# Copying the mixed V of each batch to key order: eight copies of 1 KB pieces in place of sixteen of 512 bytes

## The chip, the core and the metric

The kernel runs on one core of a Trainium2 chip. The metric is the device time of one execution in microseconds (us). Thirteen runs of the kernel before gave a median of 159.22 us, from 157.39 to 160.86. The engines are named as in the profile: PE multiplies matrices, PEld loads its weights, DVE, ACT and POOL work on vectors, SP issues transfers. "SPq" is the queue of SP.

## The reference, cut to what matters

There are 4 batches, 8 heads, a sequence of 768 tokens in 8 blocks of 96, and heads of 64 elements. A matrix P of 8x8 for each head mixes whole blocks of K and V, attention then works inside each block, and the result goes through a gated layer.

```python
k_sorted = np.einsum('bhij,bhjcd->bhicd', P, k_b)
v_sorted = np.einsum('bhij,bhjcd->bhicd', P, v_b)
scores = scale * np.matmul(q_b, k_sb.transpose(0, 1, 2, 4, 3))
attn = softmax(scores)                       # over the 96 keys of a block
x = np.matmul(attn, v_sb)                    # then (B, S, H*D)
h = np.maximum(x @ w_in, 0.0);  u, v = halves of h
v_s = w_spatial @ normalised(v) + b_spatial
out = (u * v_s) @ w_out
```

## The kernel before, in words

A load puts one input of one batch into a tile of 128 partitions: partition p holds tokens 6p to 6p+5 of every head (the six are called g). A block i of 96 tokens is therefore 16 partitions (t) times 6 values of g.

The work is cut into steps, and one string, SCHEDULE, gives their order on PE, DVE, ACT and POOL. A step is a letter, a number, a batch, the engine that empties its result (A for ACT, D for DVE) and a PSUM tile (ps0 to ps3); `v31A1` is step v, number 3, batch 1, emptied by ACT, in ps1. Each engine takes its instructions in that order; SP has an order of its own, in which its transfers were written. The steps that matter here:

- **v** (`vmix`, L260): two matmuls mix the blocks of V for a pair of heads. ACT or DVE copies the result to the tile vm (by the helper at L235 and L237). Batch 0 does the same work in another way (steps t and B) and copies nothing on SP.
- **vb<-vm** (L277, on SP): copies of vm to vb, in which the 96 partitions are the keys of a block. Each takes one block i: 96 pieces. In vm the heads lie in two halves of four, and eight copies for a half start when both pairs of that half are mixed. The order of the pairs is 0, 2, 3, 1 in batch 1, so the half of pairs 2 and 3 goes first, with 0 and 1 after it. In batches 2 and 3 it is 3, 2, 1, 0.
- **s** (`score`, L365, exponential at L372 on ACT) and **z** (`sums`, L384, then L390 and L391 on ACT): scores and their row sums.
- **a** (`attend`, L402): matmuls of vb and the exponentials; DVE multiplies by the reciprocal sums into xt (L412). Step a11 is batch 1, number 1: it reads blocks 4 to 7 of the half with pairs 0 and 1. Steps a01, a21 and a31 follow.
- **V, U, N, S, O**: the gated layer of the batch before, interleaved with attention. S (L494) is followed by an addition on DVE (vs, L505) and a product on POOL (gt, L506); O (L535) reads the four gt.
- **Q** (`qdma`, L309 and L313): for batches 2 and 3, DVE copies q_in to qr and SP issues a transposing transfer to qT.
- **The loads** of batches 2 and 3 (L94, issued by POOL: q_in, then v_in, then k_in) start behind a small copy on POOL ("gate", L596) that waits for the first exponential of the batch before.

Around a11 the order written out is `s71-2 s51-1 S20-3 s31-0 s61-2 S00-1 s11-3 s41-0 S30-2 s21-1 z11-3 Q02-- a11-0 z31-2 z01-1 O10A3 a01-2 z21-0 O00A1 a21-3 a31-2 O20A0 V01-1`. Step S30 is number 3 of the gated layer of batch 0, whose product gt is the last of four that O10, O00 and O20 read.

SP's transfers use eight completion semaphores in turn, so that a transfer waits for the one eight places ahead of it.

Of the kernel before, what the change touches and what calls it, by code (L numbers as in the profile page):

```python
# [9 lines left out]
BF16 = mybir.dt.bfloat16  # L10
# [20 lines left out]
def kernel(  # L31
# [14 lines left out]
    B, H, S, D = q.shape  # L46
    NB = sort_net.shape[-1]
    BLK = S // NB
    G = S // 128
    TB = 128 // NB  # L50
# [6 lines left out]
    HP = H // 2  # L57
# [7 lines left out]
    att = ctx.enter_context(tc.tile_pool(name="att", bufs=2))  # L65
# [13 lines left out]
    def ps_tile(n, dt=FP32):  # L79
        return psum.tile(  # L80
            [128, 2, 512 if dt == FP32 else 1024], dt, name=f"ps{n}", tag=f"ps{n}",
        )
# [9 lines left out]
    def load_heads(x, b, name):  # L92
# [16 lines left out]
        out=a16.rearrange("p (j t) -> p j t", t=TB),  # L109
        in_=a16.rearrange("p (j t) -> p j t", t=TB),  # L110
# [6 lines left out]
        out=sel.rearrange("p i (j t) -> p i j t", t=TB),  # L117
        in_=sel.rearrange("p i (j t) -> p i j t", t=TB),
# [14 lines left out]
        out=w_in_sb.rearrange("p (j x) f -> p j (x f)", x=2),  # L133
        in_=moe_w_in.rearrange("(j p x) f -> p j (x f)", j=2, x=2),
# [98 lines left out]
    def copy(eng, out, in_):  # L233
        if eng is nc.scalar:
            nc.scalar.copy(out=out, in_=in_)  # L235
        else:
            nc.vector.tensor_copy(out=out, in_=in_)  # L237
# [10 lines left out]
    class Attention:  # L248
# [7 lines left out]
        def vmix(self, hp, eng, ps):  # L256
            t = ps_tile(ps)
            for hh in range(2):
                h = 2 * hp + hh
                nc.tensor.matmul(  # L260
                    t[:, hh, 0:G * D], lhsT=self.pd[:, h, :], rhs=v_in[self.b][:, h, :],
                    start=True, stop=True,
                )
            half, h0 = hp // 2, 2 * hp % (H // 2)
            if self.vm is None:
                self.vm = att.tile([128, 2, G, H // 2, D], BF16, name="vm", tag="vm")
            copy(
                eng,
                self.vm[:, half, :, h0:h0 + 2, :].rearrange("p g h d -> p h g d"),
                t[:, :, 0:G * D].rearrange("p h (g d) -> p h g d", g=G),  # L270
            )
            if self.vb is None:
                self.vb = att.tile([BLK, NB, 2, H // 2, D], BF16, name="vb", tag="vb")
            self.mixed.append(hp)
            if hp ^ 1 in self.mixed:
                for i in range(NB):
                    nc.sync.dma_start(  # L277
                        out=self.vb[:, i, half].rearrange("c h d -> c (h d)"),
                        in_=self.vm[i * TB:(i + 1) * TB, half].rearrange("t g h d -> t g (h d)"),
                    )  # L280

        def q_tile(self):
# [282 lines left out]
    with tc.manual_schedule(engines={ET.PE, ET.DVE, ET.Activation, ET.Pool}):  # L565
# [8 lines left out]
        for x in range(1, B):  # L574
            make_pdiag(x, nc.gpsimd, 0, H)
        nc.gpsimd.tensor_copy(
            out=b_bc.rearrange("p (g c) -> p g c", g=G),
            in_=b_nat.rearrange("p (c g) -> p g c", g=G),
        )
        for step in SCHEDULE.split():  # L580
            name, n, b = step[0], int(step[1]), int(step[2])
# [48 lines left out]
```

The softmax here doesn't subtract the row's maximum and nothing guards it: scores larger than these inputs give would overflow.

## Time and profile before

| | us |
|---|---|
| median of 13 runs | 159.22 |
| lowest, highest | 157.39, 160.86 |
| the profiled execution | 159.08 |
| its span, first to last instruction | 157.3 |
| busy: PE, DVE, ACT, POOL | 143.4, 93.8, 94.4, 49.1 |
| mean granted PE clock | 0.983 of full |

The profile is of one execution. "Idle before ... <-releaser" says what ended an engine's wait. The chain that ended last is followed back from the last instruction, at each step to what released it; a piece of it shows its start, its length and its line. DMA issues have a duration on the queue that issues them and a time from issue to landing.

### The profile page before, as it was taken

What the parts mean: (1) busy time and instruction counts of PE and PEld (TensorE: products, weight loads), DVE (VectorE), ACT (ScalarE), POOL (GpSimd) and SP (SyncE); (2) the same over time, 40 slices, a digit from 0 to 9 for tenths busy, and PEclk for the clock granted to TensorE, in tenths of its full rate; (3) what the DMA queues carried; (4) which work ended last, traced back from release to release, by engine and by line L of the source; (5) the groups of instructions that cost most, each with busy time, mean ns of one, the idle gap of its engine ahead of it and who ended that gap; (6) DMA issues with size and microseconds to landing.
All of it is one profiled execution on the core that took longest, in us unless ns stands there. A gap on an engine that the chain in (4) does not pass through costs nothing.

```text
span 157.3 us, 4205 instructions
## 1 busy us (share of the span) xinstructions
PE 143.4 (91%) x1805; PEld 81.7 (52%) x1805; DVE 93.8 (60%) x193; ACT 94.4 (60%) x141; POOL 49.1 (31%) x47
## 2 busy tenths in 40 slices
PE   0968899999999789999999999999999999999970
PEld 0336785557766334455655635456555444566430
DVE  3778976498854422475962765578643855844710
ACT  3156997599755646477986725688875445550060
POOL 7975923000078620000077440000056400007500
PEclk9999999999999968999999999999999999999997
DMA  2999999999959999954469999954510063000055
GB/s 14 190 204 211 216 272 196 201 204 205 183 55 177 213 204 165 301 226 57 72 76 207 205 195 148 356 141 61 77 27 0 6 264 139 0 4 0 0 209 193
DMA packets 27171, 23.09 MB, mean 147 GB/s; under 512 B 7504, under 2 KB 25168, under 8 KB 27024
## 3 DMA queue, kind: packets, MB, share of 16 engines
q0 software_dynamic: 13504, 12.58, 49.7%
q1 hardware_dynamic: 13504, 10.10, 27.3%
q8 instruction: 14, 0.23, 0.6%
q10 hardware_dynamic: 144, 0.13, 0.3%
q14 instruction: 5, 0.04, 0.1%
HBM read 24.78 MB, written 6.29 MB: 198 GB/s over the span
## 4 chain that ended last, share of the span: by engine, by line
PE 49%; DMA 25%; POOL 7%; SPq 7%; DVE 3%; issue 2%; ACT 2%; POOLq 1%; DVEq 0%
DMA v_in<-in_v_dram 16%; PE ps L535 12%; PE ps L478 10%; PE ps L435 10%; PE ps L494 9%; SPq L277 7%; DMA q_in<-in_q_dram 5%; DMA vb<-vm 4%; POOL gt L506 3%; PE ps L260 2%; PE ps L322 2%; DVE vs L505 2%; PE ps L402 1%; PE ps L365 1%; PE ps L521 1%
## 5 line engine op out<-in xcount | busy, mean ns | idle before, releaser
L506 POOL TENSOR_TENSOR gt<-vs,u_sb 128x768 bf16<-128x768 f32 x15 | 25.2, 1687 | 50.0 <-DVE vs L505 26.4
L494 PE MATMUL ps<-wspT,v_sb 128*128 128x384 bf16 x192 | 33.4, 327 | 0.0
L372 ACT ACTIVATE ex<-ps 96x768 bf16<-96x768 f32 x32 | 24.1, 802 | 9.3 <-PE ps L365 8.9
L505 DVE TENSOR_TENSOR vs<-ps,b_bc 128x768 f32<-128x768 f32 (+1 forms) x17 | 15.5, 910 | 20.4 <-PE ps L494 20.4
L457 DVE BATCH_NORM_STATS2 stats<-v_sb 128x6 f32<-128x512 bf16 x24 | 16.2, 675 | 13.3 <-ACT v_sb L241 13.3
L494 PEld LDWEIGHTS <-v_sb 128*128 128x128 bf16 x192 | 17.8, 98 | 12.0 <-issue 0.6
L478 PE MATMUL ps<-xt,w_in_sb 128*128 128x384 bf16 x128 | 23.0, 326 | 0.0
L535 PE MATMUL ps<-w_out_sb,gt 128*128 128x512 bf16 x88 | 22.6, 403 | 0.4
L435 PE MATMUL ps<-w_in_sb,xt 128*128 128x512 bf16 x96 | 22.4, 379 | 0.0
L235 ACT COPY o_sb<-ps 128x1024 f32<-128x1024 f32 x9 | 9.1, 1012 | 20.1 <-PE ps L535 20.1
L412 DVE TENSOR_TENSOR xt<-ps,lns 128x384 bf16<-128x384 f32 x32 | 15.8, 550 | 8.8 <-PE ps L402 8.2
L241 ACT ACTIVATE v_sb<-ps 128x1024 bf16<-128x1024 f32 (+1 forms) x15 | 12.4, 851 | 9.2 <-PE ps L435 9.2
L478 PEld LDWEIGHTS <-w_in_sb 128*128 128x128 bf16 x128 | 12.1, 98 | 8.4
L435 PEld LDWEIGHTS <-xt 128*128 128x128 bf16 x96 | 9.2, 98 | 10.6 <-DVE xt L412 0.4
L535 PEld LDWEIGHTS <-gt 128*128 128x128 bf16 x88 | 8.0, 101 | 11.8 <-POOL gt L506 2.3
L596 POOL COPY gate<-ex 1x1 bf16<-1x1 bf16 x2 | 0.4, 194 | 41.2 <-ACT ex L372 41.2
L241 ACT ACTIVATE u_sb<-ps 128x768 bf16<-128x768 f32 x14 | 11.1, 808 | 1.9 <-PE ps L478 1.5
L390 ACT ACTIVATE lns<-ps 128x384 f32<-128x384 f32 x16 | 7.8, 486 | 6.7 <-PE ps L384 6.7
L365 PEld LDWEIGHTS <-kT 64*96 64x96 bf16 x256 | 7.4, 121 | 4.7 <-issue 3.3
L365 PE MATMUL ps<-qT,kT 64*96 64x96 bf16 x256 | 9.5, 210 | 0.4 <-ACT ex L372 0.4
L237 DVE CAST kT<-ps 128x768 bf16<-128x768 f32 x10 | 9.1, 945 | 0.6 <-PE ps L322 0.6
L402 PE MATMUL ps<-ex,vb 96*32 96x96 bf16 x512 | 8.0, 207 | 1.6 <-DMA vb<-vm 1.6
(80 smaller groups left out, 161.7 us busy)
## 6 DMA issues: line engine op xcount, KB each, us to landing
out_dram<-o_sb SPq DMA_DIRECT2D x11, 512.0 KB, 4.5
q_in<-in_q_dram POOLq DMA_DIRECT2D x4, 768.0 KB, 8.5
k_in<-in_k_dram POOLq DMA_DIRECT2D x4, 768.0 KB, 16.1
v_in<-in_v_dram POOLq DMA_DIRECT2D x4, 768.0 KB, 12.1
vb<-vm SPq DMA_DIRECT2D x48, 48.0 KB, 2.6
wsp_nat<-in_moe_w_spatial_dram POOLq DMA_DIRECT2D x1, 1152.0 KB, 21.3
w_in_sb<-in_moe_w_in_dram POOLq DMA_DIRECT2D x1, 1024.0 KB, 15.6
w_out_sb<-in_moe_w_out_dram POOLq DMA_DIRECT2D x1, 512.0 KB, 30.6
```

What stands on the lines that cost most here:

```text
L241: nc.scalar.activation(out=out, in_=in_, func=AF.Relu)
L277: nc.sync.dma_start(out=self.vb[:, i, half].rearrange("c h d -> c (h d)"), in_=self.vm[i * TB:(i + 1) * TB, half].rearrange("t g h d -> t ...
L365: nc.tensor.matmul(t[0:BLK, hh, ii * BLK:(ii + 1) * BLK], lhsT=self.k[hp][rows, i * BLK:(i + 1) * BLK], rhs=self.q[hp][rows, i], start=Tru ...
L372: nc.scalar.activation(out=e.rearrange("p h i c -> p h (i c)"), in_=t[0:BLK, :, 0:NB // 2 * BLK], func=AF.Exp, scale=scale,)
L412: nc.vector.tensor_mul(out=self.xt[j][:, dh, :].rearrange("p (g i t) -> p i g t", g=G, i=NB)[:, i0:i0 + NB // 2], in0=t[:, dh, 0:HW].rearr ...
L435: nc.tensor.matmul(self.vt[n][:, x, :], lhsT=self.xt(kc)[:, g * 128:(g + 1) * 128], rhs=w_in_sb[:, kc, DH:DFF], start=(kc == 0), stop=(kc ...
L457: nc.vector.bn_stats(out=stats, in_=v_sb[:, x, :])
L478: nc.tensor.matmul(t[:, x, 0:HW], lhsT=w_in_sb[:, kc, mc * 128:(mc + 1) * 128], rhs=self.xt(kc)[:, x * HW:(x + 1) * HW], start=(kc == 0), ...
L494: nc.tensor.matmul(t[:, x, 0:HW], lhsT=self.v[g][:, mc * 128:(mc + 1) * 128], rhs=wspT[:, g, x * HW:(x + 1) * HW], start=(g == 0), stop=(g ...
L505: nc.vector.tensor_add(out=vs[:, x], in0=t[:, x, 0:HW], in1=b2[:, x])
L506: eng.tensor_mul(out=gt2[:, x], in0=vs[:, x], in1=u2[:, x])
L535: nc.tensor.matmul(t[:, x, :], lhsT=self.gt[mc][:, g * 128:(g + 1) * 128], rhs=w_out_sb[:, mc, :], start=(mc == 0), stop=(mc == FC - 1),)
```

## The change

The tile vm keeps its size, but its axes are in another order: first g, then the two halves, then the four heads of a half. For one token all eight heads then lie side by side: 512 elements of two bytes, 1 KB. Copies start when all four pairs of heads are mixed, one for each block, so a batch has 8 copies of 96 KB where it had 16 of 48 KB. In the program that is built, SP's list has 8 copies of 96 pieces of 512 elements where it had 16 of 96 pieces of 256; apart from the numbers of the tiles, the orders of PE, DVE, ACT and POOL are the same. Batch 0 is untouched.

```diff
             if self.vm is None:
-                self.vm = att.tile([128, 2, G, H // 2, D], BF16, name="vm", tag="vm")
+                self.vm = att.tile([128, G, 2, H // 2, D], BF16, name="vm", tag="vm")
             copy(
                 eng,
-                self.vm[:, half, :, h0:h0 + 2, :].rearrange("p g h d -> p h g d"),
+                self.vm[:, :, half, h0:h0 + 2, :].rearrange("p g h d -> p h g d"),
                 t[:, :, 0:G * D].rearrange("p h (g d) -> p h g d", g=G),
             )
             self.mixed.append(hp)
-            if hp ^ 1 in self.mixed:
+            if len(self.mixed) == HP:
                 for i in range(NB):
                     nc.sync.dma_start(
-                        out=self.vb[:, i, half].rearrange("c h d -> c (h d)"),
-                        in_=self.vm[i * TB:(i + 1) * TB, half].rearrange("t g h d -> t g (h d)"),
+                        out=self.vb[:, i].rearrange("c x h d -> c (x h d)"),
+                        in_=self.vm[i * TB:(i + 1) * TB].rearrange("t g x h d -> t g (x h d)"),
                     )
```

## The prediction

> **What bounds the kernel now.** I read four views, in this order. First the page's slices of the span: PE is busy in nine tenths or more almost everywhere, so a copy between tiles is worth something only where PE stands still or slows.
>
> ```profile
> PE   0968899999999789999999999999999999999970
> PEclk9999999999999968999999999999999999999997
> ```
>
> Away from both ends PE dips in one place, the 14th and 15th slices (51.1 to 59.0 us), and there the granted clock falls. Second, the chain of waits through that place:
>
> ```profile
> 42.82 1.83 SPq L277
> ...
> 49.45 6.32 DMA vb<-vm
> 55.77 0.04 issue
> 55.81 0.27 PE ps L402 x8
> 56.08 0.33 PE ps L384 x8
> 56.41 3.52 PE ps L535 x8
> 59.92 0.45 PE ps L402 x32
> ```
>
> The end of the kernel is traced back through step a01 (59.92), step O10 (56.41), the last eight matmuls of a11 (55.81) and the last copy vb<-vm of batch 1, which began to be issued at 49.45 and landed at 55.77. Ahead of it stand all sixteen issues of that batch, from 38.23 on, one of them of 1.83 us. Third, the timeline there:
>
> ```profile
> 53.04 0.35 PE L384 MATMUL ps<-ex,ones 96*32 96x384 bf16 x4
> ...
> 53.85 0.27 PE L402 MATMUL ps<-ex,vb 96*32 96x96 bf16 x8 [0.46 <-DMA vb<-vm]
> 53.95 2.28 POOL L506 TENSOR_TENSOR gt<-vs,u_sb 128x768 bf16<-128x768 f32 x1 [0.97 <-DVE vs L505]
> ...
> 55.81 0.27 PE L402 MATMUL ps<-ex,vb 96*32 96x96 bf16 x8 [0.43 <-DMA vb<-vm]
> ...
> 56.34 3.58 PE L535 MATMUL ps<-w_out_sb,gt 128*128 128x512 bf16 x8
> ```
>
> Step a11 could start at 53.39, when z11 (53.04, 0.35) is through. It waits four times, once for each of its blocks, for the last four copies. O10 then needs 3.52 us for eight matmuls; eight of the same line take 1.83 at 60.54 in the chain. Fourth, the table by stretches says why:
>
> ```profile
> core 0: us, PE busy (x) PEld busy (x) DVE busy (x) ACT busy (x) POOL busy (x), PEclk, DMA share, GB/s
> 53.00:56.40 3.40, 1.78 (x51) 0.74 (x46) 1.93 (x3) 1.81 (x4) 2.28 (x1) 1.00 1.30 209
> 56.40:59.80 3.40, 3.40 (x10) 0.94 (x8) 0.82 (x2) 1.81 (x4) 0.00 (x0) 0.50 1.30 200
> 59.80:63.20 3.40, 3.40 (x110) 1.94 (x110) 1.27 (x3) 2.72 (x4) 0.00 (x0) 1.00 1.29 168
> ```
>
> PE was busy for 1.78 of 3.40 us while it waited for the copies, then had half its clock (0.50) for 3.4 us. The copies are paid twice: in the wait, and in O10.
>
> **The change part by part.** *Issues.* The price of one issue is in the list of vb's instructions:
>
> ```profile
> L277 SPq DMA_DIRECT2D vb<-vm x48: 571/600/1827, 38.2 to 113.3; - x48
> DMA to landing us min/median/max: 2.2/2.6/6.9
> ```
>
> 0.60 us, and 0.04 between two. No copy of 1 KB pieces is in this trace, so its issue is bounded by its neighbours: 0.60 if the 96 pieces set it, 1.2 if the bytes do. The output's issues at L542 move 512 KB in 128 pieces of 4 KB with a median of 0.34 us, more bytes for less time, so I take 0.60. Below 0.57 there is no row of a copy, and no reason for one.
>
> *Start.* The copies now wait for the last of four vm copies. In batch 1 that is ACT's at 39.72, 0.82 long: 40.54, where the first half began at 38.23. Eight issues at 0.64 begin from 40.57 to 45.05. If one of them again takes 1.83 (a fetch of instructions runs in that half microsecond, 42.5 to 43), the last begins at 46.28. Before it began at 49.45.
>
> *Landing.* Between 2.2 and 6.9 us (the row above). The long ones come from the loads of batch 2: these move their first packets at 46 to 47, SP's queue then gets 3 packets between 47 and 50, and about 175 a microsecond from 51 to 54. Most of the copies are issued before that. The last lands at 47.3 (45.05 + 2.2), at the worst 53.2 (46.28 + 6.9); were the landing to double with the bytes, 58.9. I take the first two, both before a11 at 53.39. *A rule on piece size:* a packet of 512 bytes takes about 50 ns here (from 108 to 116 us, 1091 packets for 41.4% of 16 engines: 53 us). The Trainium skill ("DMA: Bandwidth & Descriptors", section "Why small descriptors are slow (HBM only)") says that transfers between SBUF and SBUF don't pay the penalty of small pieces; by that a 1 KB packet takes twice as long, the engines' work for a batch stays the same, and the piece size saves nothing. No row here decides it, and the sum holds either way: six packets an engine are 0.3 to 0.6 us a copy, no more than an issue.
>
> *What is late next.* With vb there, a11's 32 matmuls take 0.51 (the row of 32 at 94.71): 53.39 to 53.90. z31 and z01 take 0.50 (55.91), free to start when DVE and ACT have emptied their PSUM tiles at 53.87 and 53.96: done by 54.46. O10's first six matmuls, at 0.23 each (1.83 / 8), end at 55.84. Its last two need S30's product on POOL, 53.95 + 2.28 = 56.23, and that does not move: DVE's addition before it ends at 53.87 as now. PE resumes about 0.05 later, as behind POOL at 92.23, and 2 x 0.23 brings it to 56.74. a01 started at 59.92: **3.18 us earlier**, 1.69 of it O10's pace (3.52 - 1.83), 1.49 the wait. The clock should hold: from 53.0 to 56.4 PE is then busy for about 2.9 us, not 1.78.
>
> *How far it carries.* From 59.92 to 77.19 the chain is PE without a wait, so all of it moves. What doesn't move with it is early enough: v_in and k_in of batch 2 land at about 58 and 63 (issued at 45.49 and 46.36, 12.5 and 16.6 us), used at 66.56 and 70.33, less 3.18; the transposed q of batch 2 lands at 67.4 (54.80 + 12.6), used at 77.10 less 3.18. Then the chain is the load of q_in for batch 3, 8.12 us from 78.92, behind the gate that waits for batch 2's first exponential: it moves too. DVE waits for that load at 87.06 with the addition of S01 behind it, POOL for that, O21 for POOL at 92.28. In batch 2 the old copies overlap this load (issues to 81.74; 42, 70, 99 and 82 packets of SP's queue in the four microseconds from 82.5, 0.7 us of the engines). The new ones begin at 72.85 and end at 78.0, so it lands 0 to 0.7 earlier; but S31 ends on PE at 89.19, then 0.11 of gap, 0.96 on DVE, 0.07, 1.64 on POOL: 91.97 and not 92.23, so at most 0.3 of it counts. I take 0.15.
>
> *Edits at nothing.* The later start of the first half in batches 2 and 3 is hidden by scores and S steps: copies landed by about 81 and 113, needed at 89.30 and 121.36. Without those 8 us it would cost the 2.3 us that they start later. The copies into vm write runs of 64 elements as before: 0 to 0.01 each. Fewer entries in SP's queue free the transposes and outputs behind them; the transpose at 54.80 waits for qr (54.74), so nothing there. Eight semaphores in turn: the ninth transfer is no longer a copy of the same batch.
>
> **Sum.** 159.08 (span 157.3 and 1.78 around it, which stays) less 3.18 less 0.15 is 155.75. That execution lies 0.14 under the median, so 155.8 stands for a median. Its own error: 0 to 0.3 at q_in, a POOL product that takes 1.64 and not 2.28 (0.44 less, as O10's first six then end last), a wait of some tenths at a11 (0.5 more): 155.2 to 156.4.
>
> **Rivals.** *The clock still falls (17%).* O10 still has a wait of 0.44 before its last two matmuls. For it: half busy was enough for a fall here. Against: 4.68 of 4.90 us busy from 87.40 to 92.30, with the wait for POOL in it, kept 1.00. A fall costs up to 1.69: 157.5. *A rule on the clock:* the trace has gaps of under half a microsecond and a drop to 0.50. The Trainium skill ("TensorE: Matmul & The Clock Gate", section "HAM oscillation — how this bites in real kernels") puts the limit at idle gaps of over 3.4 us; by that the copies didn't cause the drop, it would stay, and the time would be 157.5. The row speaks against it: no such gap stands before 56.4.
>
> *Bytes set the issue, and the first half is now late (9%): slower.* The place is SP's list in batch 1. At p us an issue the last begins at 40.57 + 7p, plus the 1.2 of the long one, and lands 6.3 later among the loads; it beats 55.77 only while p is under 1.1. At 1.24 it lands at 56.8, 1.0 later than now: 160.1. For it: half the copies wait 2.3 us longer than now, and the queue starves from 47 to 50. Against: L542's 0.34.
>
> *Nothing to see (6%).* The build keeps eight copies, but each 1 KB could go as two packets of 512, or the loads come earlier as the queue is empty and starve the last copies as before: the last four land at 55.8 again: 159.2.
>
> **How the numbers follow.** Forecast 68%: 155.8. The range takes in its bounds with half a microsecond of scatter below, and the clock case with as much above (the thirteen runs lie within 1.8 of their median): 154.7 to 158.2; left out are slower and unchanged. A measurement of this kernel can tell about 0.5% from no change. Faster: the forecast and the clock case, 85%; within 0.5%: 6%; slower: 9%.
>
> **What would show it.** Right: 24 issues of L277 of about 0.6 us; no wait of L402 for vb; O10 in about 2.3 us with POOL's gt as its last wait; clock 1.00 from 53 to 63; a01 near 56.7; the gate of batch 3 near 75. Wrong: issues of 1.2 us, or L402 waiting behind 53.4; a clock of 0.50 anywhere but the end; PE idle between 57 and 74, where I count on none.

## The result, and the profile after

The changed kernel takes 156.30 us (median of 11 runs, 156.02 to 156.73); the kernel before has 158.99 in 48 runs by now (156.74 to 160.86). The ratio of times is 0.9893, with a 95% interval of 0.9861 to 0.9925; it compares runs within 1.5% of the fastest of their kernel, which leaves out the 22 longest of the 48, so the medians lie further apart, at 0.983. The prediction was 155.8, with 154.7 to 158.2 as its range. The profiled execution took 155.94 us, with a span of 154.2; the sum was made for 155.75.

The page's slices for PE and its clock, after:

```profile
PE   0978898999999989999999999999999999999970
PEclk9999999999999999999999999999999999999998
```

The dip in the 14th and 15th slices is all but gone, and the clock stays. The chain of waits through the same place (start, length, what):

```profile
53.04 0.97 DVE vs L505
54.01 0.07 issue
54.08 2.30 POOL gt L506
56.38 0.05 issue
56.43 0.60 PE ps L535 x2
57.03 0.46 PE ps L402 x32
```

No copy and no issue of SP is in it any more. It comes through S30's addition and product, and O10's last two matmuls wait for that product. a01 starts at 57.03, not 59.92. The timeline there:

```profile
53.17 0.35 PE L384 MATMUL ps<-ex,ones 96*32 96x384 bf16 x4
...
53.34 0.51 PE L402 MATMUL ps<-ex,vb 96*32 96x96 bf16 x32
...
54.52 1.46 PE L535 MATMUL ps<-w_out_sb,gt 128*128 128x512 bf16 x6
...
56.43 0.60 PE L535 MATMUL ps<-w_out_sb,gt 128*128 128x512 bf16 x2 [0.45 <-POOL gt L506]
```

a11 runs in one piece behind z11. In the table by stretches (columns as before: PE's busy time is the second number, the granted clock the third from the end) PE is busy for 2.78 of the 3.40 us, and the clock stays at 1.00:

```profile
53.00:56.40 3.40, 2.78 (x58) 1.33 (x56) 2.85 (x4) 3.02 (x7) 2.40 (x2) 1.00 1.32 207
56.40:59.80 3.40, 3.37 (x82) 1.62 (x86) 1.02 (x2) 2.70 (x5) 0.00 (x0) 1.00 1.30 199
```

And vb's issues (ns, least, median, most) with their landings:

```profile
L277 SPq DMA_DIRECT2D vb<-vm x24: 576/596/1290, 40.7 to 107.3; - x24
...
DMA to landing us min/median/max: 2.7/3.2/6.8
```

An issue of 96 pieces of 1 KB costs 0.596 us, one of 512 bytes 0.600. The eighth copy of batch 1 is issued from 45.9 to 46.6 and is the one that takes 6.8 us: it lands at about 52.7, some 0.6 us ahead of a11 (53.34).

### The profile page after: what moved, and what is told of

Its sections match the earlier page's. It is cut to its first block, busy times and chain, and to the rows that moved or that the text cites. A ratio compares the mean times of both kernels' runs of the same rounds, so it can differ in the third digit from the quotient of the medians.

```text
span 154.2 us, 4178 instructions
## 1 busy us (share of the span) xinstructions
PE 141.7 (92%) x1805; PEld 81.7 (53%) x1805; DVE 94.2 (61%) x193; ACT 94.2 (61%) x141; POOL 49.0 (32%) x47
## 4 chain that ended last, share of the span: by engine, by line
PE 58%; DMA 29%; POOL 4%; DVE 3%; issue 2%; POOLq 1%; DVEq 0%
DMA q_in<-in_q_dram 29%; PE ps L494 14%; PE ps L535 11%; PE ps L435 10%; PE ps L478 9%; POOL gt L506 4%; PE ps L322 2%; PE ps L365 2%; PE ps L295 2%; PE ps L402 2%; DVE vs L505 2%; PE ps L260 2%; PE ps L521 1%; POOLq L625 1%; PE ps L384 1%
## 5 line engine op out<-in xcount | busy, mean ns | idle before, releaser
L535 PE MATMUL ps<-w_out_sb,gt 128*128 128x512 bf16 x88 | 21.1, 380 | 0.6 <-POOL gt L506 0.5
L468 DVE TENSOR_SCALAR v_sb<-v_sb,mv,rstd 128x512 bf16<-128x512 bf16 x24 | 8.8, 434 | 0.6 <-ACT rstd L466 0.6
```

What stands on the lines that cost most here:

```text
L535: nc.tensor.matmul(t[:, x, :], lhsT=self.gt[mc][:, g * 128:(g + 1) * 128], rhs=w_out_sb[:, mc, :], start=(mc == 0), stop=(mc == FC - 1),)
```

## The experiments

**The theory:** all of the gain is when the copies of blocks 4 to 7 land in batch 1, ahead of a11 or among the loads of batch 2. It comes as a shorter wait (about 1.5 us) and, in most executions, as a clock that doesn't fall (about 1.7). **The main rival:** larger pieces or fewer issues save something of their own, in each batch. One measure is used for all: the time from the start of z11 to the start of a01 in the profiled execution. By the timelines it is 6.81 us before (53.04 to 59.85) and 3.79 after (53.17 to 56.96); where nothing ahead of z11 was changed, its start differs by up to 0.5 us between executions, and this leaves that out. Kernels are compared with runs of the kernel before on the same chip.

**The change in batch 1 alone, and in batches 2 and 3 alone.**

```diff
-            if hp ^ 1 in self.mixed:
+            wide = self.b == 1            # the other kernel: self.b > 1
+            if wide and len(self.mixed) == HP:
...
+            if not wide and hp ^ 1 in self.mixed:
```

(vm has the new order of axes where `wide` holds, and the old one elsewhere.)

> The change in batch 1 alone; batches 2 and 3 copy as before. Theory (the gain is the last copies of batch 1, which land ahead of a11 in place of behind the loads of batch 2): all of it but 0 to 0.3 us at the load of q_in for batch 3, so 156.2 to 156.7, no wait of L402 for vb, clock 1.00 around 57. Rival (a 1 KB piece or half the issues saves something in each batch): a third of the gain, about 158.

> The change in batches 2 and 3 alone. Theory: nothing but 0 to 0.3 us, so 158.7 to 159.3 where the clock drops, with the four waits of a11 for vb as before. Rival (something is saved in each batch): two thirds of the gain, about 157.

Measured: 156.68 (156.54 to 156.89) and 159.51 (157.75 to 160.91), beside 159.19. Batch 1 alone has the gain, 2.51 us between the medians where the change has 2.69, with 3.84 us from z11 to a01; batches 2 and 3 have none (ratio 1.005, 0.9996 to 1.0104). The rival falls. The profile of the second, by stretches, holds one thing more:

```profile
53.00:56.40 3.40, 1.80 (x52) 0.75 (x48) 1.95 (x3) 1.73 (x4) 2.35 (x2) 1.00 1.30 210
56.40:59.80 3.40, 3.35 (x52) 1.58 (x50) 1.81 (x4) 3.30 (x7) 0.00 (x0) 1.00 1.30 201
```

The waits of a11 are those of the kernel before (PE busy for 1.80 us, there 1.78), but in this execution the clock held. From z11 to a01 it took 5.12 us, 1.69 less than the 6.81 of before, and the run was the fastest of its ten. So the same wait is followed by a fall of the clock in some executions and not in others.

The kept traces suggest why. Three of them have a fall of the clock in this place: the kernel before and two kernels further down (sixteen copies after the last mix, five more copies). In each the clock falls once more at the end of the kernel, 98.99 us later (56.38 and 155.37, 56.04 and 155.03, 58.93 and 157.92), which is 29 times the 3.41 us that a fall lasts. The falls thus lie on a grid of 3.41 us, whose place differs from one execution to the next. Counted back from its own fall at the end (153.46), the grid of this execution cuts the wait in two at 54.47, and PE is busy for 79% of the 3.41 us ahead of that and 73% of those behind it. In the kernel before one piece of the grid, 52.97 to 56.38, holds all four waits, with PE busy for 52%. This is read from a few traces; no run here shifts the grid. Nor is the busy share the whole rule: 62% (52.63 to 56.04, sixteen copies after the last mix) was followed by a fall, and 50% near the start of another execution (8.88 to 12.29, the two edits of order below) was not.

**Sixteen copies of 512 bytes in another order.**

```diff
             if hp ^ 1 in self.mixed:
-                for i in range(NB):
+                for i in (4, 5, 6, 7, 0, 1, 2, 3) if self.b == 1 and half == 0 else range(NB):
```

> The kernel before, with sixteen copies of 512 bytes; only the list of the last eight copies of batch 1 begins with blocks 4 to 7, which a11 reads, and ends with 0 to 3. Theory (when these four land is all that counts): they are issued from 44.75 to 47.3, land by about 53, and most of the gain is there without fewer issues or larger pieces: 156.2 to 157.0. Rival (fewer issues and larger pieces free the transfer engines or SP's queue): 159, as before.

Measured: 156.31 (156.18 to 156.58), as fast as the change, beside 159.19. Sixteen issues take 11.88 us of SP as before, and a11 runs without a wait:

```profile
53.59 0.51 PE L402 MATMUL ps<-ex,vb 96*32 96x96 bf16 x32
```

3.78 us from z11 to a01. Neither the size nor the number of the copies is needed for the gain.

**PE kept busy while it waits.** Twenty matmuls of no use, five ahead of each block of a11:

```diff
                 i = ih * (NB // 2) + ii
+                for _ in range(5 if self.b == 1 and m == 1 else 0):
+                    nc.tensor.matmul(t[:, 0, 384:512], lhsT=ident_bf, rhs=warm_sb[:, 0:128],
+                                     start=True, stop=True)
```

> The kernel before, with five matmuls of no use (128x128, into columns of PSUM that nothing reads) in front of each of a11's four blocks, so that PE isn't idle while it waits for the copies. The waits stay, the copies land as before. Theory (half of the gain is the clock, which falls because PE is half busy in those 3.4 us): O10 runs at full pace, about 1.7 us less where the clock fell, 157.3 to 157.8, and the runs lie closer together than those of before. Rival (the clock falls for another reason, or only idle gaps of over 3.4 us make it fall): 159 or more, with the clock at 0.50 from 56.4.

Measured: 157.82, and all ten runs lie from 157.20 to 158.06. By stretches:

```profile
53.00:56.40 3.40, 3.38 (x73) 2.06 (x72) 1.95 (x3) 1.74 (x4) 2.43 (x2) 1.00 1.30 211
56.40:59.80 3.40, 3.35 (x52) 1.58 (x50) 1.81 (x4) 3.30 (x7) 0.17 (x1) 1.00 1.30 202
```

a11's blocks still start some 0.6 us apart, at 54.04, 54.63, 55.21 and 55.89; only PE is busy in between. The 48 runs of the kernel before fall in two groups, 14 from 156.74 to 157.76 and 34 from 158.57 to 160.86, with none between; of the 19 beside this kernel five lie from 157.13 to 158.02 and fourteen from 158.79 up. With the filling only the lower group is left, so it is PE's idle time in the wait that makes the upper one. That each of the 34 has the fall of the clock is inferred: of the kernel before one execution was profiled, and the mean granted clock of a whole run doesn't part the groups (beside this kernel 0.974 to 0.986 in the fourteen and 0.982 to 0.984 in four of the five). Nor is the gap between the groups there in the runs beside later experiments, some of which lie from 158.00 to 158.41.

**Sixteen copies, written after the last mix.**

```diff
-            if hp ^ 1 in self.mixed:
+            if len(self.mixed) == HP:
                 for i in range(NB):
-                    nc.sync.dma_start(out=self.vb[:, i, half]...
+                    for half in range(2):
+                        nc.sync.dma_start(out=self.vb[:, i, half]...
```

> The layout of before and sixteen copies of 512 bytes, but all of them issued only when all four pairs are mixed, block by block with both halves of a block in turn: the start of the change without its smaller number of issues. Theory (the number of issues in SP's list sets when the last copies land): block 7 is issued at about 49.5 to 51, among the loads, and lands at 56 to 57; the gain is gone, 159.0 to 160.4 where the clock falls. Rival (the later start, or which half goes first, is what helped): 156.5.

Measured: 157.03 (156.44 to 159.43), beside 158.54. This didn't do what it says. SP's list isn't the order in which the transfers are written (as the section on the kernel puts it): what can start stands first. In the built list six copies of the half that was ready come first (from 38.42), and those of the other half for blocks 4, 5, 6 and 7 stand in places 11, 12, 13 and 15, where they had 13 to 16. Accordingly the first two blocks of a11 don't wait:

```profile
53.39 0.42 PE L403 MATMUL ps<-ex,vb 96*32 96x96 bf16 x16
...
54.12 0.27 PE L403 MATMUL ps<-ex,vb 96*32 96x96 bf16 x8 [0.31 <-DMA vb<-vm]
...
55.40 0.27 PE L403 MATMUL ps<-ex,vb 96*32 96x96 bf16 x8 [1.01 <-DMA vb<-vm]
```

Seven of ten runs took 156.4 to 157.4, with a mean granted clock of 0.991 to 0.999, three 158.4 to 159.4, with 0.982 to 0.984. It says nothing on a late start; as a dose between before and after it fits the theory.

**No loads of batch 2.** Its steps read the tiles of batch 1, so part of the output comes from other inputs.

```diff
+                    if b == 1:
+                        q_in[2], v_in[2], k_in[2] = q_in[1], v_in[1], k_in[1]
+                        continue
```

> The kernel before without the loads of q, v and k of batch 2: its steps read the tiles of batch 1, so part of the output is that of other inputs. Theory (the loads of batch 2 are what makes the last copies of batch 1 take 6.3 us to land): they land in 2.2 to 3 us, at 52.5 at the latest, a11 doesn't wait and the clock stays: 155.8 to 156.5, with all sixteen issues in place. Rival (SP's sixteen issues are the limit, whatever the loads do): 159.

Measured: 156.64 (156.41 to 157.60), beside 158.54. Sixteen issues as before. The landings of vb's copies, and then a11 in the timeline:

```profile
DMA to landing us min/median/max: 2.2/2.2/6.3
```

```profile
53.29 0.51 PE L402 MATMUL ps<-ex,vb 96*32 96x96 bf16 x32
```

No wait, 3.78 us from z11 to a01. The last seven copies of batch 1, issued from 45.1 on, all land in 2.2 us; in the kernel before they took 6.3 us and more (the 6.3 here is a copy of a later batch). The loads are what the last copies waited behind.

**The changed copies, later.** Two kernels have the change's eight copies of 1 KB pieces, but later. First by moving step v11:

```diff
-        ... w00D1 v11A0 k01D2 k31A3 q01D1 k21A0 q11D2
+        ... w00D1 k01D2 k31A3 q01D1 k21A0 v11A0 q11D2
```

> The changed kernel with step v11, the last pair of V in batch 1, behind k01, k31, q01 and k21 in the order: eight copies of 1 KB pieces as in the change, but issued about 3 us later, from 43.6 to 48. Theory (only the time at which the copies of blocks 4 to 7 land counts): the last ones go into the loads of batch 2 and land at 54.5 to 56, a11 waits for them again, 157.0 to 157.8 where the clock holds and 158.5 to 160 where it falls. Rival (eight issues or 1 KB pieces are the gain in themselves): 156.3.

Measured: 159.11 (157.76 to 161.87), beside 158.83; a11 waits again, three times:

```profile
55.71 0.27 PE L402 MATMUL ps<-ex,vb 96*32 96x96 bf16 x8 [0.40 <-DMA vb<-vm]
...
56.46 0.27 PE L402 MATMUL ps<-ex,vb 96*32 96x96 bf16 x8 [0.48 <-DMA vb<-vm]
...
57.17 0.27 PE L402 MATMUL ps<-ex,vb 96*32 96x96 bf16 x8 [0.44 <-DMA vb<-vm]
```

The waits are as expected, 1.32 us in all, and from z11 to a01 it takes 4.69 us, 0.90 more than in the change, with the clock at 1.00. The time of the whole kernel can't be read: z11 itself starts at 54.84, 1.67 later than in the changed kernel, since v11 waits on PE for its PSUM tile (0.89 us). So SP was pushed back instead, by five copies that nothing reads, with PE's order as in the change:

```diff
+                if self.b == 1:
+                    unread = dram.tile([5, BLK, H * D + 128], BF16, name="unread", tag="unread", bufs=1)
+                    for i in range(5):
+                        nc.sync.dma_start(out=unread[i, :, 0:H * D], in_=...)   # the same 96 x 1 KB
                 for i in range(NB):
```

> The changed kernel with five more copies of 96 pieces of 1 KB from vm in front of those of batch 1 on SP, to a place in memory that nothing reads; the orders of the other engines are the changed kernel's. They push the eight copies of vb back by five issues, 3.2 us, into the loads of batch 2, and leave PE alone, which moving step v11 did not. Theory (the time at which blocks 4 to 7 land is what counts, at its edge: the changed kernel's last copy lands some 0.5 us ahead of a11): a11 waits for vb again for 1 to 3 us, and the time is 157.0 to 158.0 where the clock holds and 158.7 to 160 where it falls. Rival (eight issues, or 1 KB pieces, are the gain in themselves): 156.3 to 156.6.

Measured: 160.82 (160.33 to 161.22), beside 157.72: slower than the kernel before, with all of the change in it.

```profile
44.75 7.17 SPq L284 DMA_DIRECT2D vb<-vm  x8
...
56.29 0.27 PE L409 MATMUL ps<-ex,vb 96*32 96x96 bf16 x8 [2.01 <-DMA vb<-vm]
...
57.02 0.27 PE L409 MATMUL ps<-ex,vb 96*32 96x96 bf16 x8 [0.46 <-DMA vb<-vm]
...
57.72 0.27 PE L409 MATMUL ps<-ex,vb 96*32 96x96 bf16 x8 [0.43 <-DMA vb<-vm]
...
58.52 0.27 PE L409 MATMUL ps<-ex,vb 96*32 96x96 bf16 x8 [0.53 <-DMA vb<-vm]
```

3.4 us of waits and 8.58 from z11 to a01. It is beyond what was expected: the copies were 4 us later, not 3.2 (44.75 against 40.72; 0.76 of that stood ahead of the five, which begin at 41.48), their issues took 7.17 us and not 5.87, landings 7.2 us at the median and 8.3 at most, and the clock fell from 58.93 to 62.34. The five copies' own traffic may be part of that; it isn't separated. So the change can lose, as in the prediction's slower rival, but by what stands in front of the copies and not by the price of an issue. That late pieces of 1 KB cost more than late ones of 512 bytes isn't shown: with v11 later the waits were 1.32 us, in the kernel before 1.62.

**What is late next.** After the change O10 waits for S30's product on POOL, which takes 2.30 us beside DVE's copy qr where others take 1.64. Step Q02 was put behind a11, in the changed kernel and in that of sixteen reordered copies; the changed kernel itself ran beside them:

```diff
-        s41-0 S30-2 s21-1 z11-3 Q02-- a11-0 z31-2
+        s41-0 S30-2 s21-1 z11-3 a11-0 Q02-- z31-2
```

> The changed kernel with step Q02 (DVE's copy qr) behind a11 in the order, not ahead of it. Theory (O10's last two matmuls now wait for S30's product on POOL, which takes 2.29 us beside that DVE copy where others take 1.64): the product ends about 0.6 earlier, O10 waits 0.45 less, 155.8 to 156.0 against 156.3 for the changed kernel. Rival (POOL is slow there for another reason, or the transposing transfer that starts 2 us later is waited for): 156.3 or more.

> The changed kernel itself, beside the others of this list on one chip: 156.0 to 156.7, as in its first runs.

> The changed kernel with step Q02 behind a11 once more, beside the changed kernel on one chip: 0.4 to 0.6 us less than it, 155.4 to 156.1. Rival (the 155.7 of its first runs was the other chip): the same as the changed kernel.

> The kernel before, its sixteen copies of 512 bytes kept, with blocks 4 to 7 first among the last eight copies of batch 1 and step Q02 behind a11: two edits of order, none of size. Theory: as fast as the changed kernel with Q02 behind a11, 155.5 to 156.1. Rival (smaller pieces cost something in batches 2 and 3): some tenths more, 156.2 or more.

Measured: 155.68 in the first of these runs (155.40 to 156.08, beside 158.54); then, on one chip beside 158.83, the changed kernel 156.49, with Q02 moved 155.53 (155.19 to 155.97), sixteen reordered copies with Q02 moved 155.51 (155.39 to 156.76). In the first kernel:

```profile
54.24 1.65 POOL L506 TENSOR_TENSOR gt<-vs,u_sb 128x768 bf16<-128x768 f32 x1 [0.97 <-DVE vs L505]
...
54.69 1.89 PE L535 MATMUL ps<-w_out_sb,gt 128*128 128x512 bf16 x8
```

The product takes 1.65 and O10 runs through. z11 to a01 falls from 3.79 to 3.16 us, 0.63; of the 0.96 between the medians the rest is not placed (z11 started 0.33 earlier in that profile, which is within what it differs by anyway). Both kernels beat the change. The one with sixteen copies of 512 bytes does so with two edits of order and none of size.

Eight copies of all heads in pieces of 512 bytes, which would change the piece size alone, were not tried.

## Why the prediction was right, step by step

- **Issues: right.** 0.596 us for 1 KB pieces against 0.60 taken; the bound of 1.2 by bytes is out.
- **Start and landing: right, near the bad end.** 40.72 against 40.57, the last issue at 45.9 against 45.05 to 46.28, the last landing at about 52.7 against 47.3 to 53.2. The forecast took both ends as safe, though the bad one lay only 0.2 us ahead of a11; the margin came out at 0.6 us, which is partly luck, and with five more copies in front the gain turned into a loss.
- **The stall and the clock: right in mechanism and size.** The stretch from z11 to a01 shrank by 3.02 us where 3.18 was summed; most of the difference is O10's last two matmuls, which took 0.60 and not 0.46. As foreseen, their wait for POOL's product is the last one left. The split holds too: the two profiles of one wait give 1.69 to the clock (the sum had 1.69) and leave 1.33 to the wait (1.49). In the filled kernel the stretch is 4.87, 1.94 less than before.
- **How often the clock falls: not foreseen.** The sum was made for an execution with the fall. Of 48 executions of the kernel before 34 lie in the upper group, so the median moved by 2.69 us of the 3.42 that were forecast (159.22 to 155.8), but the fastest ones had only some 1.1 us to gain: from 157.4, about the middle of the lower group, to 156.3. That the execution profiled was one of the majority is luck; from one of the others the sum would have had no 1.69.
- **The load of q_in for batch 3 (0.15): right in size, not in cause.** It took 8.12 us before and 7.73 after, and O21's last matmuls start 32.13 us after a01 where they had 32.36, 0.23 earlier. But the load took 7.75 in batch 1 alone and 7.77 in the other order, with 32.12 and 32.13 to O21, and both keep sixteen copies in batch 2. So the copies of batch 2 aren't needed for it, and its cause is open.
- **The clock rival: out.** 2.78 of 3.40 us busy kept 1.00, and all twelve executions of the changed kernel lie from 155.94 to 156.73, within less than a fall's 1.69. The row decided rightly against the rule there: the Trainium skill ("TensorE: Matmul & The Clock Gate", section "HAM oscillation — how this bites in real kernels") ties the fall to idle gaps of over 3.4 us; in the profiled execution of the kernel before gaps of under 0.5 us each, with PE half busy, were enough, and with them filled the clock stayed at 1.00.
- **The rule on piece size: confirmed for these two sizes.** From 101 to 110 us 896 packets of SP's queue take 55.9% of 16 engines, 90 ns each and 102 us of engine time a MB; the 512-byte ones took 49 ns and 110 us a MB. So the Trainium skill ("DMA: Bandwidth & Descriptors", section "Why small descriptors are slow (HBM only)") holds to within 8%: the bytes count here, hardly the pieces.

## What to carry to other kernels

When a small copy is late, look first at what else its queue shares the engines with at that time, and at which pieces the next reader needs first: here the order of one list gave the whole gain of a change of layout. An idle half of PE for 3 us can cost more than the idle time, through the clock, and in some executions only; read the spread of the runs as a sign of it. A gain that hangs on landing ahead of a burst of loads has an edge: measure how far away it is.

## What the runs showed that was not expected

When the loads of batch 2 set in on POOL's queue, SP's queue all but stops in the kernel before: it got 3 packets from 47 to 50 us and 176 a microsecond from 51. In the changed kernel it wasn't stopped, only slowed: 22 to 69 packets a microsecond from 47 to 52, where it had 164 from 44 to 45. In the kernel with v11 later the copies issued from 45 to 47 us land in 3.1 at the median, those from 47 to 49 in 7.2. One execution's fall of the clock lasted 3.4 us and cost 1.69, half of its length. The bf16 copy on DVE stretched a product on POOL from 1.65 to 2.30 us.
